# Sliding-window attention and a gated feed-forward on one core: output transposes from the DMA to TensorE, stores to ScalarE's queue

## The chip, the core and the metric

The kernel runs on one core of a Trainium2 chip. The core has five engines, each with its own instruction stream: TensorE (PE, with its weight loads as PEld), VectorE (DVE), ScalarE (ACT), GpSimd (POOL) and SyncE (SP), which here only issues DMAs. The five run side by side and wait for each other by semaphores; an engine takes its own instructions in the order in which they stand. The metric is the device time of one execution in microseconds, as the median of several runs. Before the change it is 388.84 us (three runs: 385.98, 388.84, 389.90).

## What is computed

Eight batches, eight heads, 576 tokens, head size 64. Attention looks back over a window of 128 tokens with a linear bias per head; the result, 4608 tokens of width 512, goes through a gated feed-forward (512 to 2048 to 512). The reference, cut:

```python
scores = scale * np.matmul(q, k.transpose(0, 1, 3, 2))
rel = pos[:, None] - pos[None, :]
bias = slopes[:, None, None] * (-np.abs(rel))[None, :, :]
mask = (rel >= 0) & (rel < 128)
scores = np.where(mask, scores + bias[None], -1e9)
attn = np.exp(scores - scores.max(-1, keepdims=True))
attn = attn / (attn.sum(-1, keepdims=True) + 1e-09)
x = np.matmul(attn, v).transpose(0, 2, 1, 3).reshape(B * S, H * D)
h = x @ w_in
g = h * (1.0 / (1.0 + np.exp(-beta * h)))
return g @ w_out
```

## The kernel before

**Attention.** Each batch has five blocks of tokens (four of 128 rows, one of 64). `load_qk` and `load_v` issue the loads of a block on SP's queue (L92) and have POOL cast them to bf16, into `bst` (L116) or into the value buffer `vs` (L121). `T(b, sb)` transposes a block of q and k into `qkT`: for batches 0 and 1 (`NPE = 2`) by PE with a copy by DVE, for the others by two DMA transposes on SP's queue (L217). `SC(b, m, p)` makes the scores of half a batch (m) for two heads (p) on PE (L257), with ACT's exps (L270) and DVE's mask (L274). `PV(b, qb, g)` multiplies by the values on PE (L296, L300) and normalises on DVE into `xn` (L305, L306). `X(b, qb)` brings a block of outputs, transposed, into the ring `XT`: for batches 0 and 1 by PE and a copy (L323, L328), for the others by a DMA transpose on SP's queue (L319). PSUM tiles `pv`, `xt` and `tps` share two buffers; the scores `sps` have one.

**Feed-forward.** Tokens go in nine groups of 512. `HS(g, j)` is a block of four matmuls over `XT` (L340), then ACT's tanh (L345) and DVE's product (L346) into `gT`; `OS(g, i, n)` is a block of four matmuls over `gT` (L356). Each group has 16 of either. The fourth `OS` of an output tile is followed by ACT's scaling into `osb` (L362) and by the store on SP's queue (L364): 36 stores in all. `hps` has two PSUM buffers, `osb` three in SBUF.

**The order.** PE's order is written by hand: the steps of attention (the list `att`, from batch 1 on) are spread between the blocks of the groups, so that what group g+1 needs stands ahead of it (`need`); in each group the last three to five blocks, and in groups 0 and 1 also the first `lead` blocks, have none. The other engines and the queues are ordered by a scheduler when the program is built. A DMA counts its end on one of eight counters, taken in turn, and so waits for the end of the DMA that stands eight places before it in the whole program.

Of the kernel before, what the change touches and what calls it, by code (L numbers as in the profile page):

```python
# [13 lines left out]
P = 128  # L14
# [3 lines left out]
def kernel(  # L18
# [10 lines left out]
    nc = tc.nc  # L29
    B, H, S, D = q.shape  # L30
# [21 lines left out]
    REF = 64.0  # L52
    NEG = -1e12
    NPE = 2

    const = ctx.enter_context(tc.tile_pool(name="const", bufs=1))
    diff = const.tile([P, P], F32, name="diff")
# [13 lines left out]
    XT = const.tile([P, NDM, XTR], BF16, name="XT")  # L71
# [48 lines left out]
    def load_v(b, sb):  # L120
        return nc.gpsimd.tensor_copy(  # L121
            out=VS[b % 2][0 : ROWS[sb], sb, :, 0:D], in_=load_rows(v, b, sb)
        )
# [88 lines left out]
    def T(b, sb):  # L212
        rows = ROWS[sb]
        src = staged.pop((b, sb))
        if b >= NPE:
            for i in range(2):
                nc.sync.dma_start_transpose(  # L217
                    out=QK[b % 2][:, i, :, P * sb : P * sb + rows],
                    in_=src[0:rows, i].rearrange("r h d -> r (h d)"),
                )  # L220
            return
        tps = psum_t.tile([P, 2, NP, P], BF16, name="tps", tag="t")
        for i in range(2):
            for p in range(NP):
                nc.tensor.transpose(
                    out=tps[:, i, p, :],
                    in_=src[:, i, 2 * p : 2 * p + 2, :].rearrange("r h d -> r (h d)"),
                    identity=ident[:],
                )
        nc.vector.tensor_copy(  # L230
            out=QK[b % 2][:, :, :, P * sb : P * sb + rows], in_=tps[:, :, :, 0:rows]
        )
# [78 lines left out]
    def X(b, qb):  # L311
        nq = ROWS[qb]
        xnv = xns.pop((b, qb))[:].rearrange("p h d -> p (h d)")
        tok0 = (b * S + P * qb) % XTR
        n1 = min(nq, XTR - tok0)
        parts = [(tok0, 0, n1)] + ([(0, n1, nq)] if n1 < nq else [])
        if b >= NPE:
            for at, r0, r1 in parts:
                nc.sync.dma_start_transpose(out=XT[:, :, at : at + r1 - r0], in_=xnv[r0:r1, :])  # L319
            return  # L320
        xt = psum_t.tile([P, NDM, P], BF16, name="xt", tag="t")
        for c in range(NDM):
            nc.tensor.transpose(  # L323
                out=xt[:, c, :], in_=xnv[:, c * P : (c + 1) * P], identity=ident[:]
            )
        copy = nc.vector.tensor_copy if b else nc.scalar.copy
        for at, r0, r1 in parts:
            copy(out=XT[:, :, at : at + r1 - r0], in_=xt[:, :, r0:r1])  # L328
# [21 lines left out]
    def OS(g, i, n):  # L350
        gT = gts[g]
        if n == 0:
            opss[g, i] = psum_o.tile([P, DM], F32, name="ops", tag="ops")
        ops_ = opss[g, i]
        for j in range(4 * n, 4 * n + 4):
            nc.tensor.matmul(  # L356
                ops_[:], lhsT=gT[:, j, i * P : i * P + P], rhs=W2[:, j, :],
                start=(j == 0), stop=(j == NFF - 1),
            )
        if n == 3:  # L360
            osb = osb_pool.tile([P, DM], F32, name="osb", tag="osb")
            nc.scalar.mul(osb[:], ops_[:], 0.5)  # L362
            row0 = g * TOKG + i * P
            nc.sync.dma_start(out=out[row0 : row0 + P, :], in_=osb[:])  # L364


    def merged(a, c):
        n, ia, ic, r = max(len(a), len(c)), 0, 0, []
        for s in range(n):
            while ia < len(a) and ia * n <= s * len(a):  # L370
                r.append(a[ia])
                ia += 1
            while ic < len(c) and ic * n <= s * len(c):
                r.append(c[ic])
                ic += 1
        return r

    def pvx(b, qbs):
        r = []
        for qb in qbs:  # L380
            r += [(None, lambda g=g, qb=qb: PV(b, qb, g)) for g in range(2)]
            if qb != qbs[0]:
                r.append(((b, qb - 1), lambda qb=qb: X(b, qb - 1)))
        r.append(((b, qbs[-1]), lambda: X(b, qbs[-1])))
        return r

    def loads(b, m):

        if b + 1 < B:
            for sb in HALF[m]:  # L390
                load_qk(b + 1, sb)
        if m == 0:
            for sb in (2, 3, 4):
                load_v(b, sb)
        elif b + 1 < B:
            for sb in (0, 1):
                load_v(b + 1, sb)

    HALF = ((0, 1, 2), (3, 4))

    def ts(b, m):
        return [(None, lambda sb=sb: T(b, sb)) for sb in HALF[m]]

    def scs(b, m):
        return [(None, lambda p=p: SC(b, m, p)) for p in range(NP)]
# [5 lines left out]
    att, before = one, []  # L411
    for b in range(2, B):
        for m in range(2):
            nb, nm = (b, 1) if m == 0 else (b + 1, 0)
            if nb < B:
                att += ts(nb, nm)
            att.append((None, lambda b=b, m=m: loads(b, m)))
            att += merged(scs(b, m), before)
            before = pvx(b, ((0, 1), (2, 3, 4))[m])
    att += before  # L420
    place = {key: n + 1 for n, (key, _) in enumerate(att) if key}

# [6 lines left out]
    with tc.manual_schedule(engines={mybir.EngineType.PE}):  # L429

        for sb in range(NQB):
            c = load_v(0, sb)
            if sb == 3:
                with tc.issue_after(c.ins):
                    load_w1(0)
                    load_w1(1)
        for sb in range(3):
            c = load_qk(1, sb)
            if sb:
                with tc.issue_after(c.ins):  # L440
                    load_w1(sb + 1)
        for sb in range(2):
            load_v(1, sb)
        for sb in (3, 4):
            load_qk(1, sb)
        for sb in (2, 3, 4):
            c = load_v(1, sb)
            if sb == 3:
                with tc.issue_after(c.ins):
                    for n in range(4):  # L450
                        load_w2(n)
        with tc.tile_pool(name="psum_x", bufs=2, space=bass.MemoryType.PSUM) as psum_x:
            nsc = 0
            values = [(qb, 0) for qb in range(NQB)]
            for p in range(NP + 1):
                if p < NP:
                    T0(p)
                if p == 1:
                    load_beta()
                if p:  # L460
                    for m in range(2):
                        SC(0, m, p - 1, psum_s if nsc % 3 == 2 else psum_x)
                        nsc += 1
                        if p == NP:
                            PV(0, *values.pop(0))
            for qb, g in values:
                PV(0, qb, g)
        psum_h = ctx.enter_context(
            tc.tile_pool(name="psum_h", bufs=2, space=bass.MemoryType.PSUM))
        psum_o = ctx.enter_context(  # L470
            tc.tile_pool(name="psum_o", bufs=2, space=bass.MemoryType.PSUM))
        for qb in range(NQB):
            c = PV(0, qb, 1)
            if qb:
                X(0, qb - 1)
        X(0, NQB - 1)
        with tc.issue_after(c.ins):
            late_consts()
        for sb in HALF[0]:
            load_qk(2, sb)  # L480
        for sb in (0, 1):
            load_v(2, sb)
        done = 0
        for g in range(NTG):
            items = []
            for j in range(NFF):
                items.append(lambda g=g, j=j: HS(g, j))
                if g > 1:
                    items.append(lambda g=g, j=j: OS(g - 1, j // 4, j % 4))
            if g == 1:  # L490
                for sb in HALF[1]:
                    load_qk(2, sb)
                for _, t in ts(2, 0):
                    t()
                items += [lambda j=j: OS(0, j // 4, j % 4) for j in range(NFF)]
            target = need[g + 1] if g + 1 < NTG else len(att)
            lead = (1, 12)[g] if g < 2 else 0
            start, span_ = done, len(items) - lead - (0 if g == 0 else 5)
            for n, it in enumerate(items):
                it()  # L500
                to = start + (target - start) * (n + 1 - lead) // span_
                while done < min(target, to):
                    att[done][1]()
                    done += 1
        for j in range(NFF):
            OS(NTG - 1, j // 4, j % 4)
# [30 lines left out]
```

## Time and profile before

| | |
|---|---|
| median of three runs | 388.84 us |
| the profiled execution | 389.58 us, its span 387.4 us, mean granted clock 0.932 |
| PE busy | 325.7 us (84% of the span), 2161 matmuls recorded |
| ACT busy | 212.0 us (55%) |
| DVE busy | 187.8 us (48%) |
| POOL busy | 84.7 us (22%) |
| moved by DMA | 52.98 MB, 160222 packets, 149424 of them under 512 B |
| SP's and ACT's queues | 120 loads, 60 score transposes, 31 output transposes and 36 stores on SP's; one load on ACT's |

The span goes from the first to the last instruction; the profiled time lies 2.2 us above it. Busy shares are means over a run with different stages, so the lines that matter are those of a stretch. In the profile, "A <- B" after an idle time names what A waited for. SPq is SP's DMA queue; time there is the time that SP takes to issue. Some matmul records are missing (558 and 555 of 576 each).

### The profile page before, as it was taken

How to read it: one execution, taken by the hardware profiler on the slowest of the kernel's cores; microseconds unless marked ns; L12 is line 12 of the kernel's file. 1: busy time of each engine (PE TensorE's matmuls, PEld its weight loads, DVE VectorE, ACT ScalarE, POOL GpSimd, SP SyncE). 2: the span in 40 equal slices, each digit the busy share in tenths (PEclk: the TensorE clock that was granted, in tenths of full speed). 3: DMA queues.
4: the chain of work that ended last, by engine and by line, in shares of the span. 5: the costliest groups of instructions: out<-in, count | busy, mean ns of one | idle time of the engine just before them, and what ended most of it. 6: DMA issues, size and time to landing. Idle time of an engine off the chain costs nothing.

```text
span 387.4 us, 6060 instructions
## 1 busy us (share of the span) xinstructions
PE 325.7 (84%) x2161; PEld 152.4 (39%) x2201; DVE 187.8 (48%) x409; ACT 212.0 (55%) x407; POOL 84.7 (22%) x139
## 2 busy tenths in 40 slices
PE   3978898767640799989969993899999999999996
PEld 1454454323310244434424441344444445444442
DVE  5474577635210356735635672175666745444310
ACT  3645665677220378656736782277778754445421
POOL 7633623205224132304231242230000000000000
PEclk9979999989685699999999998699999999999999
DMA  7999999869869798949997698983212111201012
GB/s 228 221 212 212 169 192 207 113 129 178 153 141 235 155 196 161 195 98 201 199 186 163 112 239 161 154 164 76 54 60 59 49 34 45 71 28 54 29 55 81
DMA packets 160222, 52.98 MB, mean 137 GB/s; under 512 B 149424, under 2 KB 155584, under 8 KB 160192
## 3 DMA queue, kind: packets, MB, share of 16 engines
q1 hardware_dynamic: 155936, 48.39, 63.5%
q0 software_dynamic: 4224, 4.19, 6.7%
q8 instruction: 17, 0.28, 0.4%
q14 instruction: 13, 0.11, 0.1%
q10 hardware_dynamic: 32, 0.01, 0.0%
HBM read 36.71 MB, written 9.44 MB: 119 GB/s over the span
## 4 chain that ended last, share of the span: by engine, by line
PE 59%; DMA 22%; SPq 14%; issue 2%; POOL 2%; ACT 0%; DVE 0%; POOLq 0%; ACTq 0%
PE ops L356 27%; PE hps L340 25%; DMA fst<-in_v_dram 10%; SPq L92 8%; DMA fst<-in_q_dram 6%; SPq L217 5%; DMA XT<-xn 4%; PE sps L257 3%; DMA fst<-in_k_dram 2%; PE pv L300 2%; PE pv L296 1%; POOL vs L121 1%; SPq L102 1%; SPq L364 1%; POOL bst L116 0%
## 5 line engine op out<-in xcount | busy, mean ns | idle before, releaser
L340 PE MATMUL hps<-XT,W 128*128 128x512 bf16 x558 | 149.2, 391 | 33.1 <-DMA XT<-xn 30.7
L345 ACT ACTIVATE sig<-hps,beta_h 128x512 bf16<-128x512 f32 x144 | 99.6, 692 | 112.1 <-PE hps L340 104.8
L346 DVE SCALAR_TENSOR_TENSOR gT<-sig,hps 128x512 bf16<-128x512 bf16 x144 | 98.5, 684 | 110.9 <-ACT sig L345 110.4
L356 PE MATMUL ops<-W,gT 128*128 128x512 bf16 x555 | 145.0, 388 | 1.4 <-issue 0.9
L340 PEld LDWEIGHTS <-W 128*128 128x128 bf16 x576 | 53.1, 100 | 94.5 <-issue 42.9
L270 ACT ACTIVATE pt<-sps,bias 128x256 bf16<-128x256 f32 (+1 forms) x192 | 75.3, 478 | 24.4 <-PE sps L257 24.2
L356 PEld LDWEIGHTS <-gT 128*128 128x128 bf16 x576 | 53.3, 99 | 60.2 <-issue 5.9
L116 POOL CAST bst<-fst 128x512 bf16<-128x512 f32 (+1 forms) x70 | 44.5, 641 | 146.7 <-DMA fst<-in_q_dram 108.8
L274 DVE TENSOR_TENSOR pt<-pt,mask 128x1024 bf16<-128x1024 bf16 x48 | 34.7, 723 | 22.8 <-ACT pt L270 22.4
L257 PE MATMUL sps<-qkT 64*128 64x256 bf16 (+2 forms) x320 | 27.1, 262 | 11.2 <-DMA qkT<-bst 6.1
L306 DVE TENSOR_TENSOR xn<-pv,zs 128x256 bf16<-128x256 f32 (+1 forms) x80 | 33.7, 422 | 2.5
L121 POOL CAST vs<-fst 128x512 bf16<-128x512 f32 (+1 forms) x40 | 26.0, 652 | 28.4 <-DMA fst<-in_v_dram 27.6
L362 ACT ACTIVATE osb<-ops 128x512 f32<-128x512 f32 x36 | 21.7, 602 | 19.1 <-PE ops L356 18.8
L305 DVE RECIPROCAL zs<-pv 128x4 f32<-128x4 f32 (+1 forms) x80 | 14.2, 177 | 34.8 <-PE pv L300 33.7
L300 PE MATMUL pv<-vs,pt 128*128 128x65 bf16 x320 | 29.6, 197 | 0.2 <-DVE xn L306 0.2
L257 PEld LDWEIGHTS <-qkT 64*128 64x128 bf16 x320 | 11.5, 95 | 40.0 <-issue 35.1
L296 PE MATMUL pv<-vs,pt 128*128 128x65 bf16 x256 | 25.0, 198 | 2.2 <-DVE xn L306 1.7
L300 PEld LDWEIGHTS <-pt 128*128 128x128 bf16 x320 | 22.7, 100 | 9.5 <-issue 0.6
L296 PEld LDWEIGHTS <-pt 128*128 128x128 bf16 x256 | 20.5, 101 | 10.3 <-DVE xn L306 3.4
L265 ACT ACTIVATE pt<-sps 128x1024 bf16<-128x1024 f32 x16 | 15.9, 1025 | 10.7 <-PE sps L257 10.4
L243 PE MATMUL sps<-table,sident 128*128 128x512 bf16 x31 | 10.2, 411 | 1.3 <-ACT pt L265 1.1
L206 DVE COPY qkT<-tps 128x512 bf16<-128x512 bf16 x8 | 5.5, 689 | 7.7 <-PE tps L200 7.7
(41 smaller groups left out, 60.1 us busy)
## 6 DMA issues: line engine op xcount, KB each, us to landing
out_dram<-osb SPq DMA_DIRECT2D x36, 256.0 KB, 2.5
fst<-in_q_dram SPq DMA_DIRECT2D x32, 256.0 KB, 4.6
fst<-in_k_dram SPq DMA_DIRECT2D x32, 256.0 KB, 4.8
fst<-in_v_dram SPq DMA_DIRECT2D x32, 256.0 KB, 5.1
W<-in_moe_w_in_dram POOLq DMA_DIRECT2D x4, 512.0 KB, 8.1
W<-in_moe_w_out_dram POOLq DMA_DIRECT2D x4, 512.0 KB, 11.8
fst<-in_q_dram SPq DMA_DIRECT2D x8, 128.0 KB, 4.2
fst<-in_k_dram SPq DMA_DIRECT2D x8, 128.0 KB, 4.3
```

What stands on the lines that cost most here:

```text
L92: nc.sync.dma_start(out=f[0:rows], in_=src[b, :, P * sb : P * sb + rows, :].rearrange("h p d -> p h d"),)
L116: c = nc.gpsimd.tensor_copy(out=t[0 : ROWS[sb], i], in_=load_rows(src, b, sb))
L257: nc.tensor.matmul(o, lhsT=qk[64 * e : 64 * e + 64, 1, p, P * kb : P * kb + P], rhs=qk[64 * e : 64 * e + 64, 0, p, P * kb : P * kb + nq], ...
L270: nc.scalar.activation(out=pt[:, e, cols], in_=sps[:, e, cols], func=ACTF.Exp, scale=qscale, bias=bias[:, half, h : h + 1],)
L274: nc.vector.tensor_tensor(out=pt[:], in0=pt[:], in1=masks[m][:].rearrange("p (o c) -> p o c", o=1).broadcast_to([P, 2, 512]), op=ALU.mult,)
L296: nc.tensor.matmul(pv[:, hl, 0 : D + 1], lhsT=weights(b, qb - 1, h, 1), rhs=vs[:, qb - 1, h, 0 : D + 1], start=True, stop=False,)
L300: nc.tensor.matmul(pv[:, hl, 0 : D + 1], lhsT=weights(b, qb, h, 0), rhs=vs[:, qb, h, 0 : D + 1], start=qb == 0, stop=True,)
L306: return nc.vector.tensor_tensor(out=xn[0:nq, 4 * g : 4 * g + 4, :], in0=pv[0:nq, :, 0:D], in1=zs[0:nq].broadcast_to([nq, 4, D]), op=ALU.mult,
L340: nc.tensor.matmul(hps[:], lhsT=W1[:, c, bass.ts(j, P)], rhs=XT[:, c, c0 : c0 + TOKG], start=(c == 0), stop=(c == NDM - 1),)
L345: nc.scalar.activation(out=sig[:], in_=hps[:], func=ACTF.Tanh, scale=beta_h[:, j : j + 1])
L346: nc.vector.scalar_tensor_tensor(out=gts[g][:, j, :], in0=sig[:], scalar=1.0, in1=hps[:], op0=ALU.add, op1=ALU.mult)
L356: nc.tensor.matmul(ops_[:], lhsT=gT[:, j, i * P : i * P + P], rhs=W2[:, j, :], start=(j == 0), stop=(j == NFF - 1),)
```

## The change

- `X` uses PE's transposes and a DVE copy for every batch. The DMA branch is gone.
- `T` uses PE for batches 0 to 2 (`NTE = 3`). Batch 2's `T` steps move into the list `att`, merged with its scores, and are no longer issued ahead of group 1's blocks.
- The stores are issued by ACT.
- `loads(b, 0)` issues the last three value blocks of batch b ahead of the q and k of batch b+1.
- The steps of batch 2 end before batch 3's scores begin. `lead` of group 1 is 8 for 12, and the tail without attention is 3 blocks for 5.

```diff
+    NTE = 3
...
-        if b >= NPE:
+        if b >= NTE:
             for i in range(2):
                 nc.sync.dma_start_transpose(
...
-        if b >= NPE:
-            for at, r0, r1 in parts:
-                nc.sync.dma_start_transpose(out=XT[:, :, at : at + r1 - r0], in_=xnv[r0:r1, :])
-            return
         xt = psum_t.tile([P, NDM, P], BF16, name="xt", tag="t")
...
-            nc.sync.dma_start(out=out[row0 : row0 + P, :], in_=osb[:])
+            nc.scalar.dma_start(out=out[row0 : row0 + P, :], in_=osb[:])
...
+        if m == 0:
+            for sb in (2, 3, 4):
+                load_v(b, sb)
         if b + 1 < B:
             for sb in HALF[m]:
                 load_qk(b + 1, sb)
-        if m == 0:
-            for sb in (2, 3, 4):
-                load_v(b, sb)
-        elif b + 1 < B:
-            for sb in (0, 1):
-                load_v(b + 1, sb)
+            if m == 1:
+                for sb in (0, 1):
+                    load_v(b + 1, sb)
...
-            if nb < B:
+            if NTE <= nb < B:
                 att += ts(nb, nm)
             att.append((None, lambda b=b, m=m: loads(b, m)))
-            att += merged(scs(b, m), before)
+            att += merged((ts(b, m) if b < NTE else []) + scs(b, m), before)
             before = pvx(b, ((0, 1), (2, 3, 4))[m])
+        if b < NTE:
+            att += before
+            before = []
...
-                for _, t in ts(2, 0):
-                    t()
...
-            lead = (1, 12)[g] if g < 2 else 0
-            start, span_ = done, len(items) - lead - (0 if g == 0 else 5)
+            lead = (1, 8)[g] if g < 2 else 0
+            start, span_ = done, len(items) - lead - (0 if g == 0 else 3)
```

Line numbers of the new kernel differ by one to three: the loads are L93, DMA score transposes L218, PE's X transposes L320, tanh L342, scaling L359, stores L361.

**SP's queue around batch 3's scores.** Before, from the last transposes of batch 3's q and k (`qkT_74`) to the output transpose that group 2 needs first (rows are DMAs in the order of issue; `fst` is the staging of a load):

```order
L217 DMA_TRANSPOSE qkT_74<-bst 128x4x64 x2
L92 DMA fst<-in_q_dram 128x8x64
L364 DMA out_dram<-osb 128x512
L92 DMA fst<-in_k_dram 128x8x64
L92 DMA fst<-in_q_dram 128x8x64
L92 DMA fst<-in_k_dram 128x8x64
L92 DMA fst<-in_q_dram 128x8x64
L92 DMA fst<-in_k_dram 128x8x64
L92 DMA fst<-in_v_dram 128x8x64 x2
L92 DMA fst<-in_v_dram 64x8x64
L319 DMA_TRANSPOSE XT<-xn 128x4x128
```

The same queue now, from the first transpose of batch 3's q and k to the values behind the last:

```order
L218 DMA_TRANSPOSE qkT_74<-bst 128x4x128 x5
L93 DMA fst<-in_q_dram 128x8x64
L218 DMA_TRANSPOSE qkT_74<-bst 128x4x128
L93 DMA fst<-in_k_dram 128x8x64
L93 DMA fst<-in_q_dram 64x8x64
L93 DMA fst<-in_k_dram 64x8x64
L93 DMA fst<-in_v_dram 128x8x64 x2
L218 DMA_TRANSPOSE qkT_74<-bst 128x4x128 x2
L218 DMA_TRANSPOSE qkT_74<-bst 128x4x64 x2
L93 DMA fst<-in_v_dram 128x8x64 x2
L93 DMA fst<-in_v_dram 64x8x64
```

The store and the output transpose no longer stand between the loads; in the whole program SP's DMAs go from 247 to 170: the 120 loads stay, and 50 of the 60 score transposes.

**ACT's order around the second store.** Before (`pt<-sps` are exps of a score tile, `osb<-ops` the scaling; the waits are those on the engines' and DMAs' counters):

```order
L362 ACTIVATE osb<-ops 128x512 [waits PE_49]
L270 ACTIVATE pt<-sps,bias 128x320 [waits PE_49]
L270 ACTIVATE pt<-sps,bias 128x192
L270 ACTIVATE pt<-sps,bias 128x320
L270 ACTIVATE pt<-sps,bias 128x192
```

And now:

```order
L359 ACTIVATE osb<-ops 128x512 [waits PE_49]
L271 ACTIVATE pt<-sps,bias 128x320 [waits PE_49]
L361 DMA out_dram<-osb 128x512 [waits DMAHW2_49,Activation_49]
L271 ACTIVATE pt<-sps,bias 128x192
L271 ACTIVATE pt<-sps,bias 128x320
L271 ACTIVATE pt<-sps,bias 128x192
```

The store stands between the exps of one score tile. It waits for a DMA counter (`DMAHW2`), and with it the exps behind it. The DMA that used this counter last, eight places before, is one of SP's: for the first store a load of batch 3's fifth block, for the second a score transpose of that block, for the fifteenth a load of batch 7, the 13th from the end of SP's 170 DMAs. From the sixteenth on it is a store.

## The prediction

> **What bounds the kernel now.** I began with the page's forty slices, cut the run into three stretches, and then read the waits of TensorE (PE), the timeline around the longest one, and the rows of the queue that PE waits for.
>
> ```profile
> PE   3978898767640799989969993899999999999996
> PEclk9979999989685699999999998699999999999999
> DMA  7999999869869798949997698983212111201012
> ```
>
> ```profile
> 74.50:129.00 54.50, 25.61 (x171) 11.74 (x175) 13.61 (x29) 19.14 (x46) 15.82 (x24) 0.76 0.95 168
> 129.00:262.00 133.00, 118.72 (x785) 53.39 (x799) 70.77 (x144) 81.08 (x169) 34.56 (x53) 0.93 0.89 169
> 262.00:387.40 125.40, 120.83 (x714) 56.23 (x726) 58.25 (x111) 68.84 (x128) 0.61 (x1) 0.99 0.17 52
> ```
>
> Columns of the stretches: span, busy time of PE, weight loads, DVE, ACT and POOL, granted clock, busy share of the DMA engines, GB/s. From 262 us on PE is busy for 120.83 of 125.40 us at clock 0.99: there PE is the bound, and the other engines keep up. Before that it is idle for 28.9 us in the first stretch and 14.3 us in the second, at a lower clock, while the DMA share is about 0.9. So the time to be won lies between 74 and 262 us.
>
> ```profile
> PE hps L340 <- DMA XT<-xn: 30.7, 4, 17.6
> PE sps L257 <- DMA qkT<-bst: 6.1, 3, 2.7
> PE sps L257 <- ACT pt L270: 4.7, 5, 1.7
> ```
>
> ```profile
> 108.86 5.09 SPq L217 DMA_TRANSPOSE qkT<-bst  x4
> 114.01 0.58 SPq L92 DMA_DIRECT2D fst<-in_q_dram  x1
> ...
> 120.50 3.50 SPq L92 DMA_DIRECT2D fst<-in_v_dram  x3
> ...
> 124.09 1.25 SPq L319 DMA_TRANSPOSE XT<-xn  x1
> ...
> 128.20 1.86 PE L340 MATMUL hps<-XT,W 128*128 128x512 bf16 x4 [17.57 <-DMA XT<-xn]
> ```
>
> (Waits: total us, times, longest; timeline: start, us.) Four waits make 30.7 us: the first matmul of a token group waits for a transposed attention output. In the longest, 17.57 us, the transpose was issued on SP's queue at 124.09, behind four score transposes, a store and nine loads, issued one after the other from 108.86 on. The data was there; the queue was not free.
>
> ```profile
> L217 SPq DMA_TRANSPOSE qkT<-bst x60: 1186/1206/2297, 67.7 to 255.0; - x60
> L319 SPq DMA_TRANSPOSE XT<-xn x20: 1214/1253/1652, 106.2 to 260.8; - x20
> L364 SPq DMA_DIRECT2D out_dram<-osb x17: 373/561/1584, 104.5 to 260.1; - x17
> L92 SPq DMA_DIRECT2D fst<-in_v_dram x28: 433/702/2218, 87.8 to 259.4; - x28
> L92 SPq DMA_DIRECT2D fst<-in_k_dram x26: 425/607/1856, 66.8 to 247.7; - x26
> L92 SPq DMA_DIRECT2D fst<-in_q_dram x25: 425/578/1292, 82.1 to 246.4; - x25
> DMA to landing us min/median/max: 3.1/4.3/6.9
> 67.00:262.00 195.00, 0.89 0.91 168
> 67.72 14.37 SPq L217 DMA_TRANSPOSE qkT<-bst  x10
> ```
>
> These are SP's issues between 67 and 262 us (min/median/max ns; the landing row is that of the loads). At their medians they take 60 x 1.206 + 20 x 1.253 + 17 x 0.561 + 28 x 0.702 + 26 x 0.607 + 25 x 0.578 = 157 of 195 us, and with the long ones most of the rest: SP issues nearly without a pause. The last two rows: the DMA engines are busy for 0.91 of that time, and batch 2's ten score transposes alone hold SP for 14.37 us.
>
> **The change part by part.** *Attention outputs off the DMA.* The 30 X steps of batches 2 to 7 no longer use SP, so the four waits go: -30.7. What could be late instead is DVE's copy, but the order places each X some three blocks of PE work ahead of the group that needs it.
>
> *Batch 2's transposes on PE.* SP saves the 14.37 us, so batch 3's transposes start that much earlier, and the waits of scores for qkT go with them: -6.1 (at the least half, if batch 3 is late again: -3). The five ACT waits of the third row above (4.7) stay; four scores now stand between tanh steps of group 1, so ACT gives 0.69 more to each; I take +1.
>
> *The clock.* After a long wait PE runs its first blocks slowly:
>
> ```profile
> 243.84 1.87 PE hps L340 x4
> 245.70 1.71 PE ops L356 x4
> 247.41 1.71 PE hps L340 x4
> 249.12 1.05 PE ops L356 x4
> ...
> 373.69 10.11 PE ops L356 x46
> ```
>
> A block of four matmuls takes 0.86 us when PE runs freely (the last row: (10.11 - 0.38)/45 = 0.216 each). The four blocks after the wait at 243.84 took 6.34, 2.9 too many. Two other waits (128.20 and 200) have the same tail, and the score waits near 98 a shorter one: -8, between -5 and -10.
>
> *The price on PE.* 30 x 4 + 5 x 8 = 160 transposes.
>
> ```profile
> 32.48 1.06 PE L225 MATMUL tps<-ident,bst 128*128 128x128 bf16 x16
> 72.52 0.39 PE L323 MATMUL xt<-ident,xn 128*128 128x128 bf16 x4
> L225 PE MATMUL tps<-ident,bst x40: 219/219/230, 31.2 to 43.4; 128*128 128x128 bf16 x40
> L328 DVE COPY XT<-xt x5: 283/411/424, 51.6 to 73.2; 128x512 bf16<-128x512 bf16 x4, 128x256 bf16<-128x256 bf16 x1
> L230 DVE COPY qkT<-tps x5: 417/690/692, 31.8 to 43.6; 128x1024 bf16<-128x1024 bf16 x4, 128x512 bf16<-128x512 bf16 x1
> ```
>
> One takes 219 ns by itself, but they overlap: sixteen took 1.06 us, so a further one costs (1.06 - 0.22)/15 = 56 ns, and four in 0.39 say the same. 160 x 0.056 = +9.0, all of it on the path, since PE is to be the bound. The Trainium skill speaks against this: its page "TensorE: Matmul & The Clock Gate", section "Part 4: PE-mode transpose", gives about 275 ns for a transpose inside a kernel. By that the term would be 160 x 0.275 = 44 and the sum 35 higher; the sixteen in 1.06 us decide for 56 ns here. DVE gets 30 x 0.41 + 5 x 0.69 = 15.8 us of copies; in the second stretch it was busy for 70.77 of 133, so they fit: 0.
>
> *Stores on ACT.* SP saves 17 x 0.56 = 10 us. ACT pays for 36 issues.
>
> ```profile
> L140 ACTq DMA_DIRECT2D bflat<-in_moe_beta_dram x1: 438/438/438, 0.7 to 0.7; - x1
> L362 ACT ACTIVATE osb<-ops x36: 597/598/624, 88.2 to 383.9; 128x512 f32<-128x512 f32 x36
> 227.66 0.60 ACT L362 ACTIVATE osb<-ops 128x512 f32<-128x512 f32 x1
> ```
>
> ACT's only DMA issue took 0.438, SP's stores 0.56 at the median: about 18 us in all. ACT is busy for 81.08 of 133, so most of it fits into gaps; behind a store stand exps and tanhs for which PE waits. If the first 15 stores, which fall among exps, delay PE in full, that is 15 x 0.56 = 8; if none does, 0. I take +2, since PE has two buffers there.
>
> *A new wait on ACT.* By the order a store also waits for the DMA eight places earlier, which is now on another queue. If SP is behind, ACT stands still, and then PE. The fifteenth store is the last that waits for a load; that load is the 13th from the end of SP's 170 DMAs. Where is PE then? Before, that store's osb began at 227.66; less the three XT waits up to there (22.5), 6.1 and 5 of clock, plus 15 X and 5 T (5.6): about 200. Where is SP? It needs 195 - 14.4 - 25.1 - 9.5 = 146 us for what is left, so the load is issued at about 67 + 0.9 x 146 = 198 and lands at 203. Bounds: without the long issues 50 transposes x 1.206 + 79 loads x 0.63 = 110, so 67 + 99 + 4 = 170, no wait; if the DMA engines are the limit, 0.91 x 195 = 177 us of work, less a tenth for the transposes taken away (about 3.5 MB of 168 x 0.195 = 32.8), gives 160 and 67 + 144 + 4 = 215, 15 late. Lateness doesn't add up over the stores, it is the largest one that PE pays. A small one comes at once: batch 3's loads are near the first store too. +5, between 0 and 15.
>
> *Values ahead of scores.* Three loads of batch 2 go before six of batch 3: the latter start 3 x 0.7 = 2 us later, but SP is 14 us ahead by then: 0.
>
> Sum on the span of 387.4: -30.7 - 6.1 + 1 - 8 + 9.0 + 2 + 5 = 359.6. The profiled run lies 2.2 above its span and 0.7 above the median of the runs, so I predict 361 us.
>
> **The rivals.**
> (1) *All cover holds*: no new wait, ACT's issues free: 361 - 7 - 3 = 351. For it: SP loses a third of its issues. Against it: the DMA share of 0.91.
> (2) *The DMA engines, not SP, set the pace of the loads*: the stores hold ACT for the full 15, and some of the 8 is paid: 361 + 10 + 5 = 376. For it: the same 0.91.
> (3) *Transposes don't overlap.* With matmuls around them, each could cost PE its whole 219 ns: 160 x 0.219 = 35 in place of 9, and if PE must also wait for the 30 copies because two PSUM buffers serve pv, xt and tps, 30 x 0.41 = 12 more: 399, slower. It decides from 27 us above my sum, that is from 56 + 27000/160 = 225 ns for each. Against it: the four in 0.39 stood between other matmuls. The skill's 275 ns (the page above) would do the same alone: 361 + 35 = 396.
> (4) *The gain is given back*: PE reaches the scores of later batches before their transposes are ready, and XT waits become qkT waits. Behind batch 7's first scores the order has some 430 block matmuls and that batch's attention: 430 x 0.216 + 7 = 100 us. For 385 SP's last transposes would have to land at about 280, later than before (255). With SP's end at 67 + 146 = 213, or 67 + 177 = 244 at its old pace, this sets no limit.
>
> **How the numbers follow.** Main case, 355 to 370: 0.60, predicted 361. Rival 1: 0.10; rival 2: 0.20; rival 3: 0.05; rival 4: 0.05. The range 350 to 379 takes in rival 1's 351 and rival 2's 376 and leaves out 3 and 4 and the edges. About 1% is what a measurement of this kernel tells from no change: faster is under 385.0, slower over 392.7. Faster: 0.60 + 0.10 + 0.20 = 0.90; same 0.05 (rival 4); slower 0.05 (rival 3).
>
> **What would show it.** Right: no wait of hps for a DMA; group 2's first matmul near 104 instead of 128.20; SP's last load near 215 instead of 259; clock near 1 from 75 on; transposes 56 ns apart. The new wait shows as idle ACT between an osb and the exp behind its store, ended by a load. I am wrong if PE stays idle for more than 20 us between 75 and 262, if transposes stand over 200 ns apart, or if hps waits for DVE's XT copies.

## The result and the profile after

The changed kernel takes 369.04 us (median) against 389.37: ratio 0.9486, 95% interval 0.9381 to 0.959. The forecast was 361 with a range of 350 to 379. The direction and the range held, and the time lay 8 us above the forecast. The medians count every execution; the ratio leaves out one slow one on either side (372.41 and 392.04 us). The profiled execution took 370.02 us, its span is 368.2.

These lines are from the page of the new kernel: three of the forty-slice lines (9.2 us a slice) and the group of PE's first feed-forward matmuls (busy us, mean ns, idle before them).

```profile
PE   2978597979698399999998999999999999999995
PEclk9999899989899599999999999999999999999999
DMA  7999999997897999999998934000001100011011
...
L337 PE MATMUL hps<-XT,W 128*128 128x512 bf16 x554 | 146.8, 386 | 3.9 <-DVE gT L343 1.7
```

The same group on the page of the kernel before:

```profile
L340 PE MATMUL hps<-XT,W 128*128 128x512 bf16 x558 | 149.2, 391 | 33.1 <-DMA XT<-xn 30.7
```

The idle time before `hps` falls from 33.1 us to 3.9, and a DMA no longer ends it. The holes in PE's line from the 15th slice on are gone. Behind the first batches two deep ones are left, in the 11th and the 14th slice, and there the clock falls too. The list of waits names what is behind them (total us, times, longest):

```profile
PE sps L258 <- ACT pt L271: 14.2, 6, 6.5
ACT pt L271 <- DMA fst<-in_k_dram: 12.4, 3, 5.8
```

The second row is ACT, about to do exps, ended by a load. ACT does not use that load; only the counter of the stores connects the two. Here is ACT's timeline around the first and the fifth store (start and duration in us, in brackets the idle time before):

```profile
88.65 0.60 ACT L359 ACTIVATE osb<-ops 128x512 f32<-128x512 f32 x1 [2.85 <-PE ops L353]
92.73 0.37 ACTq L361 DMA_DIRECT2D out_dram<-osb  x1
93.15 1.57 ACT L271 ACTIVATE pt<-sps,bias 128x320 bf16<-128x320 f32 x4 [3.91 <-DMA fst<-in_k_dram]
...
117.49 0.62 ACT L359 ACTIVATE osb<-ops 128x512 f32<-128x512 f32 x1
123.50 0.34 ACTq L361 DMA_DIRECT2D out_dram<-osb  x1
123.89 1.57 ACT L271 ACTIVATE pt<-sps,bias 128x256 bf16<-128x256 f32 x4 [5.77 <-DMA fst<-in_k_dram]
```

and PE's at the same places:

```profile
90.31 1.04 PE L353 MATMUL ops<-W,gT 128*128 128x512 bf16 x4
...
94.77 0.40 PE L258 MATMUL sps<-qkT 64*128 64x256 bf16 x6 [3.18 <-ACT pt L271]
...
96.24 1.90 PE L353 MATMUL ops<-W,gT 128*128 128x512 bf16 x4
98.07 0.61 PE L258 MATMUL sps<-qkT 64*128 64x256 bf16 x6
98.61 1.51 PE L353 MATMUL ops<-W,gT 128*128 128x512 bf16 x4
...
108.30 1.03 PE L337 MATMUL hps<-XT,W 128*128 128x512 bf16 x4
...
117.67 0.39 PE L258 MATMUL sps<-qkT 64*128 64x256 bf16 x4 [0.94 <-ACT pt L271]
...
125.50 0.61 PE L258 MATMUL sps<-qkT 64*128 64x256 bf16 x4 [6.47 <-ACT pt L271]
126.05 1.89 PE L353 MATMUL ops<-W,gT 128*128 128x512 bf16 x4
127.87 0.61 PE L258 MATMUL sps<-qkT 64*128 64x256 bf16 x4
128.41 1.89 PE L337 MATMUL hps<-XT,W 128*128 128x512 bf16 x4
130.09 1.15 PE L353 MATMUL ops<-W,gT 128*128 128x512 bf16 x4
```

An output tile is scaled, its store then stands still on ACT, the exps behind it stand with it, and PE waits for the exps because the scores have one PSUM buffer. The three gaps are 3.18 + 0.94 + 6.47 = 10.6 us. The slow rows behind them, each against the 1.04 and 0.39 of the same form at full clock, add 0.86 + 0.22 + 0.47 = 1.6 and 0.22 + 0.85 + 0.22 + 0.85 + 0.11 = 2.3. Together that is 14.5 us by this trace alone. The clock shows in three stretches after the second wait (us of PE, PEld, DVE, ACT and POOL with counts, then clock, DMA share, GB/s):

```profile
124.00:128.00 4.00, 2.50 (x10) 0.69 (x11) 1.53 (x3) 3.60 (x9) 1.82 (x3) 0.50 0.89 181
128.00:132.00 4.00, 4.00 (x17) 1.49 (x14) 1.83 (x3) 2.25 (x5) 0.62 (x1) 0.71 0.87 180
132.00:136.00 4.00, 3.95 (x34) 1.82 (x34) 2.26 (x6) 3.35 (x8) 2.48 (x4) 1.00 1.34 208
```

A gap in one trace is not yet a loss: it counts only as far as PE would not have waited there without the stores on ACT. That, and what each other part is worth, the runs have to tell.

### The profile page after: what moved, and what is told of

It reads as the page before. It is cut to its first block, busy times and chain, and to the rows that moved or that the text cites. A ratio compares the mean times of both kernels' runs of the same rounds, so it can differ in the third digit from the quotient of the medians.

```text
span 368.2 us, 6281 instructions
## 1 busy us (share of the span) xinstructions
PE 329.0 (89%) x2318; PEld 159.1 (43%) x2361; DVE 199.9 (54%) x445; ACT 211.6 (57%) x407; POOL 83.8 (23%) x139
## 4 chain that ended last, share of the span: by engine, by line
PE 41%; DMA 31%; SPq 20%; POOL 3%; issue 2%; ACT 0%; DVE 0%; ACTq 0%; POOLq 0%
PE ops L353 20%; PE hps L337 16%; DMA fst<-in_k_dram 15%; SPq L93 13%; DMA fst<-in_v_dram 11%; SPq L218 6%; DMA fst<-in_q_dram 6%; PE sps L258 2%; POOL bst L117 2%; POOL vs L122 1%; SPq L103 1%; PE pv L301 1%; PE xt L320 1%; PE pv L297 1%; POOL W L170 1%
## 5 line engine op out<-in xcount | busy, mean ns | idle before, releaser
L337 PE MATMUL hps<-XT,W 128*128 128x512 bf16 x554 | 146.8, 386 | 3.9 <-DVE gT L343 1.7
L342 ACT ACTIVATE sig<-hps,beta_h 128x512 bf16<-128x512 f32 x144 | 98.9, 691 | 87.9 <-PE hps L337 71.1
L337 PEld LDWEIGHTS <-W 128*128 128x128 bf16 x576 | 51.6, 99 | 59.1 <-issue 9.5
L353 PEld LDWEIGHTS <-gT 128*128 128x128 bf16 x576 | 52.4, 99 | 56.2 <-issue 4.5
L275 DVE TENSOR_TENSOR pt<-pt,mask 128x1024 bf16<-128x1024 bf16 x48 | 33.9, 705 | 24.7 <-ACT pt L271 24.6
L258 PE MATMUL sps<-qkT 64*128 64x256 bf16 (+2 forms) x320 | 26.7, 262 | 14.6 <-ACT pt L271 14.2
L359 ACT ACTIVATE osb<-ops 128x512 f32<-128x512 f32 x36 | 21.7, 603 | 25.1 <-PE ops L353 24.9
L258 PEld LDWEIGHTS <-qkT 64*128 64x128 bf16 x320 | 11.5, 96 | 43.4 <-issue 41.9
L301 PE MATMUL pv<-vs,pt 128*128 128x65 bf16 x320 | 28.4, 194 | 0.2 <-DVE xn L307 0.2
L297 PE MATMUL pv<-vs,pt 128*128 128x65 bf16 x256 | 23.9, 193 | 2.6 <-DVE xn L307 2.2
L301 PEld LDWEIGHTS <-pt 128*128 128x128 bf16 x320 | 21.5, 97 | 9.3 <-DVE xn L307 0.3
L297 PEld LDWEIGHTS <-pt 128*128 128x128 bf16 x256 | 19.6, 98 | 9.9 <-DVE xn L307 3.6
L266 ACT ACTIVATE pt<-sps 128x1024 bf16<-128x1024 f32 x16 | 15.9, 1025 | 11.2 <-PE sps L258 11.1
L325 DVE COPY XT<-xt 128x512 bf16<-128x512 bf16 (+1 forms) x36 | 13.6, 386 | 10.4 <-PE xt L320 10.3
L320 PE MATMUL xt<-ident,xn 128*128 128x128 bf16 x160 | 15.3, 219 | 1.0 <-DVE xn L307 0.7
```

The lines of the kernel that those rows point to most:

```text
L258: nc.tensor.matmul(o, lhsT=qk[64 * e : 64 * e + 64, 1, p, P * kb : P * kb + P], rhs=qk[64 * e : 64 * e + 64, 0, p, P * kb : P * kb + nq], ...
L275: nc.vector.tensor_tensor(out=pt[:], in0=pt[:], in1=masks[m][:].rearrange("p (o c) -> p o c", o=1).broadcast_to([P, 2, 512]), op=ALU.mult,)
L297: nc.tensor.matmul(pv[:, hl, 0 : D + 1], lhsT=weights(b, qb - 1, h, 1), rhs=vs[:, qb - 1, h, 0 : D + 1], start=True, stop=False,)
L301: nc.tensor.matmul(pv[:, hl, 0 : D + 1], lhsT=weights(b, qb, h, 0), rhs=vs[:, qb, h, 0 : D + 1], start=qb == 0, stop=True,)
L337: nc.tensor.matmul(hps[:], lhsT=W1[:, c, bass.ts(j, P)], rhs=XT[:, c, c0 : c0 + TOKG], start=(c == 0), stop=(c == NDM - 1),)
L342: nc.scalar.activation(out=sig[:], in_=hps[:], func=ACTF.Tanh, scale=beta_h[:, j : j + 1])
```

## The experiments

Theory A: the transposes took SP's queue off PE's path as forecast, and the new wait of the stores on ACT gave some 14 us back. Rivals: the issues on ACT cost by themselves (B), or the loads are limited by the DMA engines and would hold up something else anyway. Each run states its median and its ratio to the kernel before, which took 389.1 to 389.4 us beside them.

**Stores back on SP, or on POOL.**

```diff
-            nc.scalar.dma_start(out=out[row0 : row0 + P, :], in_=osb[:])
+            nc.sync.dma_start(out=out[row0 : row0 + P, :], in_=osb[:])
```

> The changed kernel with the stores back on SP, all else kept. Theory A (the missing 8 us went into two waits of ACT: a store on ACT holds the exps behind it until a load of SP's queue has landed, 3.18 and 6.47 us of PE): the two waits are gone, SP gets some 15 stores between loads (0.56 each) but PE's data were far ahead, so 355 to 365 us, and no exp waits for a load. Rival B (the loads come too late whoever issues the stores): PE waits as long at other places, 367 to 373. Rival C (the stores' move was a real part of the gain): SP is late again, 372 to 382.

The second kernel has `nc.gpsimd` in the same place; by the order of the program its stores count on other counters than the loads.

> Stores issued by POOL, whose DMAs count on other counters than SP's. Theory A: no exp waits for a load; the two gaps of PE go (9.6 us and the slow blocks behind them), 354 to 362 us, if POOL's casts behind a store are not late. Rival B (loads too late anyway): 366 to 373. Rival D: POOL, waiting for osb, holds casts and through them SP's transposes: 370 to 385, and PE waits for qkT or vs.

Measured: 354.44 us (0.9101, 0.9019 to 0.9183) on SP and 354.96 (0.9103, 0.9038 to 0.9168) on POOL. Both are some 14 us faster than the change as made. The stretches of the run with stores on SP:

```profile
74.50:104.00 29.50, 25.11 (x217) 13.43 (x221) 16.06 (x36) 17.06 (x41) 10.71 (x15) 1.00 0.82 162
104.00:129.00 25.00, 22.53 (x159) 10.53 (x161) 15.44 (x32) 19.45 (x44) 8.63 (x14) 1.00 0.96 188
129.00:200.00 71.00, 70.38 (x506) 33.59 (x514) 45.48 (x96) 48.61 (x100) 20.04 (x30) 1.00 0.96 182
```

and the same stretches of the change as made:

```profile
74.50:104.00 29.50, 23.83 (x176) 11.46 (x179) 15.85 (x33) 16.66 (x39) 10.51 (x16) 0.88 0.88 180
104.00:129.00 25.00, 17.49 (x118) 7.87 (x119) 9.00 (x20) 10.09 (x22) 8.87 (x14) 0.82 0.94 186
129.00:200.00 71.00, 68.17 (x483) 32.43 (x490) 41.70 (x88) 46.53 (x97) 21.02 (x34) 0.99 1.11 191
```

With the stores on SP the clock is 1.00 from 74.5 to 200 us, and PE gets 376 matmuls done between 74.5 and 129 us where it got 294. The DMA share is 0.82 to 0.96, against 0.88 to 1.11 in the change; yet from 60 us on no DMA and no issue on SP's queue stands in the chain of work that ended last. So the loads are not what limits this kernel.

PE does the same work in the same order in both traces, so its rows can be set side by side. These are the starts of the same five blocks of scores, in us:

| block of scores | change | stores on SP | lag of the change |
|---|---|---|---|
| before the wait at the first store | 89.98 | 87.00 | 2.98 |
| after it | 100.39 | 93.66 | 6.73 |
| before the wait at the fifth store | 117.67 | 110.94 | 6.73 |
| after it | 132.90 | 118.93 | 13.97 |
| after the fifteenth store | 228.27 | 210.50 | 17.77 |

The first 3 us stand before any store and are not the stores' doing. The wait at the first store then costs 3.7 us, the one at the fifth 7.2, and 3.8 more are lost between 133 and 228 us: 14.8 us in all, where the medians say 14.6. The first two waits thus cost 11.0 us and not the 14.5 of the gaps and slow rows above, because with the stores on SP PE waits for exps too, also at these places: 0.45 and 0.62 us at the first, the same 0.94 ahead of the fifth, and twice 0.69 behind it. Its list of waits and one of these rows:

```profile
PE sps L258 <- ACT pt L271: 6.7, 8, 1.9
...
93.66 0.40 PE L258 MATMUL sps<-qkT 64*128 64x256 bf16 x6 [0.62 <-ACT pt L271]
```

Two different issuing engines give the same time, so what counts is not that SP has the stores, but that ACT has not. The Trainium skill, page "DMA: Bandwidth & Descriptors", section "Issuing engines are not separate DMA queues", says that issuing from several engines saves only the sequencer time of the issue. The runs agree as far as SP and POOL go (354.4 and 355.0); what ACT's stores cost is a wait that this section does not speak of.

**Only some of the stores on ACT.** Two kernels split the 36 stores: the first 16 on SP and 20 on ACT, or the first 8 on ACT and 28 on SP.

```diff
+            (nc.sync if g < 4 else nc.scalar).dma_start(out=out[row0 : row0 + P, :], in_=osb[:])
```

> The first 16 stores (groups 0 to 3) are issued by SP again, the other 20 by ACT. Theory A (the changed kernel loses its 14.6 us because ACT's early stores wait for the counter of one of SP's loads or transposes; issuing by itself costs nothing): the later stores find few of SP's DMAs ahead of them, so 353 to 358 us, and no PE gap above 3 us. Rival B (an issue on ACT costs PE its 0.34 us and the delay of the exps or tanhs behind it): 20 of 36 stores still pay, so 14.6 x 20/36 = 8 us stay: 361 to 364. A store between 200 and 215 us can still meet one of SP's last loads under A: that would show as one gap, at most 5 us.

```diff
+            (nc.scalar if g < 2 else nc.sync).dma_start(out=out[row0 : row0 + P, :], in_=osb[:])
```

> Only the first 8 stores (groups 0 and 1) are issued by ACT, the other 28 by SP; all else as changed. Theory A (the loss of the changed kernel comes from those of its stores that meet a counter of SP's late DMAs; its two long PE gaps, 3.2 us at 92 and 6.5 us at 119, stand behind its first and fifth store, with slow blocks after them): most of the 14.6 us is already lost with these 8, so 364 to 370 us. Rival B (every issue on ACT costs about the same, 14.6/36 = 0.4 us): 354.4 + 8 x 0.4 = 357 to 358.

Measured: 358.66 us (0.9219, 0.9163 to 0.9275) and 368.35 (0.9468, 0.9424 to 0.9512). By the medians the first eight stores alone carry 13.9 of the 14.6 us, with intervals of some 2 and 3 us either way on the two times. Of the twenty late ones, the first costs, and the others don't show: this is ACT's timeline in the kernel with twenty on ACT,

```profile
215.78 0.60 ACT L359 ACTIVATE osb<-ops 128x512 f32<-128x512 f32 x1 [0.42 <-PE ops L353]
220.86 0.38 ACTq L361 DMA_DIRECT2D out_dram<-osb  x1
221.34 0.69 ACT L342 ACTIVATE sig<-hps,beta_h 128x512 bf16<-128x512 f32 x1 [4.97 <-DMA fst<-in_v_dram]
```

and PE behind it:

```profile
223.54 0.39 PE L258 MATMUL sps<-qkT 64*128 64x256 bf16 x4 [3.21 <-ACT pt L271]
223.87 1.59 PE L337 MATMUL hps<-XT,W 128*128 128x512 bf16 x4
...
225.71 1.90 PE L353 MATMUL ops<-W,gT 128*128 128x512 bf16 x4
```

It is the gap that was foreseen under A: one wait for one of SP's last loads, 3.21 us of PE and slow rows behind it. (A had said 358 at most and no gap above 3 us; both were passed by a little.) Against the kernel with all stores on SP this trace falls back by 5 us at this wait and by nothing after it; the medians differ by 4.2. Nothing is left for the other nineteen issues: B falls. In the kernel with eight on ACT the two waits are those of the change again:

```profile
PE sps L258 <- ACT pt L271: 14.2, 6, 6.2
ACT pt L271 <- DMA fst<-in_k_dram: 9.9, 2, 5.5
```

Set beside the kernel with stores on SP, its trace loses 5.0 and 6.1 us at these two waits, 0.4 at the eighth store, and nothing behind the later ones, which SP issues. The change, with ACT issuing these too, loses 3.8 us from the eighth store on. So the first eight stores cost some 11.5 us and the next six the rest; the medians are too coarse to show this split.

**Outputs by DMA again**, once with the stores on ACT as changed, once with the stores on SP:

```diff
+        if b >= NPE:
+            for at, r0, r1 in parts:
+                nc.sync.dma_start_transpose(out=XT[:, :, at : at + r1 - r0], in_=xnv[r0:r1, :])
+            return
```

> Outputs of batches 2 to 7 again by DMA transposes on SP; batch 2's q and k on PE, stores on ACT and the order of the loads as changed. My account of the gain (-30.7 and most of the slow clock for X, +7 for its 120 transposes on PE) gives a loss of some 20 to 25 us against the changed kernel: 385 to 395, with PE waiting for XT again. Rival (the gain came from SP's queue being shorter by stores and ten transposes, so that XT would come in time anyway): 365 to 375.

> Stores on SP, and the attention outputs of batches 2 to 7 by DMA transpose again; batch 2's scores on PE and the order of the loads stay as changed. Theory A (X on PE is what takes away most of the waits, since SP's queue was the limit): SP again carries 30 transposes x 1.25 = 38 us plus 36 stores, and hps waits for XT: 375 to 390 us, 20 to 35 above the 354 of the kernel with stores on SP. Rival C (with batch 2's transposes off SP the queue is already fast enough and XT waits were a matter of batch 2 alone): PE saves its 120 x 0.056 = 7 us and pays some XT waits: 350 to 362.

Measured: 375.93 us (0.9617, 0.953 to 0.9703) and 375.62 (0.967, 0.9608 to 0.9731). The first was a miss: only 7 us above the change, not 16 to 26. The second shows why. With X by DMA it makes no difference where the stores are: PE waits for SP's queue in any case, either at `hps` or behind ACT. With the stores on SP the waits are at `hps`:

```profile
PE hps L341 <- DMA XT<-xn: 24.5, 3, 10.4
```

The outputs on PE are thus worth 7 us while ACT's stores wait (375.9 to 369.0) and 21 us when they don't (375.6 to 354.4).

**Batch 2's scores by DMA again**, with the stores on ACT and on SP:

```diff
-    NTE = 3
+    NTE = 2
...
+                for _, t in ts(2, 0):
+                    t()
```

> Batch 2's q and k again by ten DMA transposes on SP, issued ahead of group 1 as before; outputs on PE and stores on ACT as changed. My account: SP is 14 us later from 67 us on, the stores on ACT meet loads that are later still, so ACT's waits grow: 375 to 385. Rival (batch 2's part is worth only its 6 us of score waits less 2 us of transposes on PE): 370 to 375.

> Stores on SP, batch 2's scores of q and k transposed by DMA again, outputs on PE. Theory A (batch 2's ten DMA transposes put SP 14 us back and PE waits for qkT near 98 us and after): 6 waits of scores minus 40 x 0.056 = 2.2 us on PE and some cold clock: 358 to 364 us. Rival (X on PE gives SP enough room, those transposes are hidden): 352 to 355.

Measured: 373.59 us (0.9586, 0.9501 to 0.9671) and 355.91 (0.9141, 0.9091 to 0.9191). Theory A expected 375 or more of the first and 358 or more of the second. The first came out in its rival's range (370 to 375), the second 0.9 us above its rival's (352 to 355). With outputs on PE and stores on SP the ten DMA transposes of batch 2 are nearly hidden: 1.5 us, which the intervals don't tell from zero. The waits of scores that were 6.1 us before are

```profile
PE sps L258 <- DMA qkT<-bst: 2.4, 2, 1.6
```

**The transposes of the outputs done twice** from batch 3 on, stores on SP. The kernel does these 100 transposes a second time into the same place.

```diff
-        for c in range(NDM):
+        for c in list(range(NDM)) * (2 if b > 2 else 1):
```

> Stores on SP, and the PE transposes of the outputs of batches 3 to 7 are done twice (25 blocks x 4 = 100 further transposes, the same result). By 56 ns for each: 5.6 us more than 354.4, 359 to 361. By the 219 ns that one takes alone: 22 more, 375 to 378. By 275 ns: 27 more, 380 to 383. If there is slack on PE at those places: 354 to 356.

Measured: 358.15 us (0.9221, 0.9163 to 0.928), 3.7 above 354.44, or 37 ns for each; the two intervals, some 3 us each, allow the 5.6 us of 56 ns and not the 22 of 219. The traces are finer: the score block at 110.94 us with stores on SP starts at 111.62 here, and the two spans end at 349.9 and 356.2. The lag grows from 0.7 to 6.3 us over the hundred, which is 56 ns for each. Its timeline shows eight in a row, where the change has four in 0.39:

```profile
264.99 0.61 PE L320 MATMUL xt<-ident,xn 128*128 128x128 bf16 x8
```

```profile
L320 PE MATMUL xt<-ident,xn x160: 216/219/230, 23.3 to 319.9; 128*128 128x128 bf16 x160
271.38 0.39 PE L320 MATMUL xt<-ident,xn 128*128 128x128 bf16 x4
```

That is (0.61 - 0.39)/4 = 55 ns for a further one, in the midst of the feed-forward, though each takes 219 by itself.

**One edit of the kernel before at a time**: the outputs of all batches on PE, or the stores on ACT.

```diff
-        if b >= NPE:
-            for at, r0, r1 in parts:
-                nc.sync.dma_start_transpose(out=XT[:, :, at : at + r1 - r0], in_=xnv[r0:r1, :])
-            return
```

> The kernel before with one edit: the outputs of all batches are transposed on PE. Theory (SP's queue was the limit and the 30 output transposes on it were what PE waited for): the 30.7 us of waits of hps for XT go, 8 of slow clock behind them too, 120 transposes cost 6.7: 389.1 - 30.7 - 8 + 6.7 = 357, so 354 to 362. Rival (the gain is given back: the waits of scores for batch 2's and 3's qkT, 6.1 us before, grow since PE comes earlier while SP still issues all 60 score transposes): 363 to 375.

```diff
-            nc.sync.dma_start(out=out[row0 : row0 + P, :], in_=osb[:])
+            nc.scalar.dma_start(out=out[row0 : row0 + P, :], in_=osb[:])
```

> The kernel before with one edit: the stores are issued by ACT. Theory D (one lateness of SP's queue, paid once: where hps waits for XT anyway, ACT's wait for an SP counter falls into the same time, as with outputs by DMA on either side of the stores, 375.9 and 375.6 us): 383 to 392. Rival E (the wait on ACT adds up to the other): 389.1 + 14.6 = 400 to 406.

Measured: 356.95 us (0.918, 0.9136 to 0.9224) and 387.56 (0.9958, 0.9919 to 0.9997). The first edit alone brings 32.4 us, nearly all that any kernel here won and more than the whole change. Its waits of scores for transposes are down to

```profile
PE sps L257 <- DMA qkT<-bst: 2.0, 1, 2.0
```

without batch 2 having been touched. The second edit costs nothing in the kernel before: there its wait falls into a time in which PE waits anyway. Its waits show that ACT is held there too, and that `hps` waits correspondingly less for XT (30.7 before):

```profile
PE hps L340 <- DMA XT<-xn: 18.8, 3, 9.2
...
PE sps L257 <- ACT pt L270: 16.3, 7, 8.6
```

**The old order of loads**, stores on SP (the last three value blocks go behind the q and k of the next batch again):

```diff
-        if m == 0:
-            for sb in (2, 3, 4):
-                load_v(b, sb)
         if b + 1 < B:
...
+        if m == 0:
+            for sb in (2, 3, 4):
+                load_v(b, sb)
+        elif b + 1 < B:
```

> Stores on SP and the loads in the old order (the last three value blocks behind the q and k of the next batch); all else as changed. Theory (the order of these loads was costed at nothing): 353 to 357 us, the same as the 354.4 with the new order. Rival (values late, so PV waits for vs): 358 to 364.

Measured: 353.74 us (0.9079, 0.903 to 0.9127), the same as 354.44 within the intervals. These two are the best kernels of the study: the change without its stores on ACT, in either order of the loads.

The worth of the two moves off SP's queue, by four kernels with stores on SP:

| | outputs by DMA | outputs on PE |
|---|---|---|
| batch 2's scores by DMA | 389.4 (the kernel before) | 357.0 |
| batch 2's scores on PE | 375.6 | 354.4 |

(The lower row has the new order of loads and the new `lead` and tail as well; with those and batch 2 by DMA, outputs on PE give 355.9. With outputs by DMA no run separates batch 2's move from them.) Either move wins more where it is made first, 13.8 and 32.4 us, than after the other, 2.6 and 21.2: 11.2 us of lateness are taken away by both.

## Why the prediction came near, and what failed

*Attention outputs off the DMA, -30.7.* Right. No wait of `hps` for a DMA is left. The edit alone brought 32.4 us; its own terms, -30.7 - 8 of clock + 120 x 0.056 = 6.7, give -32.0.

*Batch 2's transposes, -6.1 + 1 and 2.2 of PE.* The waits went, but not by this step. They fell to 2.0 us as soon as the outputs left the queue. After that the step was worth 1.5 us in place of some 3 forecast. With the stores on ACT it was worth 4.6. The waits of scores for exps, 4.7 us before and forecast at 1 more, are 6.7 with the stores on SP.

*The clock, -8.* Right where nothing holds PE: 1.00 in the three stretches from 74.5 to 200 us with the stores on SP, above. In the change it is 0.88 and 0.82 up to 129, because the new waits have slow rows behind them, as the old ones had.

*160 transposes at 56 ns, +9.0.* Right: 55 ns from eight in a row, and the hundred doubled ones cost 5.6 us between the traces (3.7 between the medians). Neither 219 ns (22 us) nor the 275 ns that the Trainium skill, page "TensorE: Matmul & The Clock Gate", section "Part 4: PE-mode transpose", gives for one inside a kernel (27.5 us for the hundred) is what a further transpose costs here. DVE's copies cost nothing: with the stores on SP `hps` waits once for one of them, 1.1 us, as it did before.

*Stores on ACT, +2 for the issues, nothing lost on SP.* The issues cost too little to be seen (19 of 20 late stores leave no trace), so this was nearer 0. That SP gains 10 us was worth nothing: with the stores back on SP its last load is issued at 217.0 us in place of 212.8, and the kernel is 14.6 us faster.

*The new wait on ACT, +5, between 0 and 15.* This is the term that was mis-sized: taking the stores off ACT again won 14.6 us. That is the upper end of the range, but not for the reason given, so that the range held is in part luck. I asked how late SP would be at the fifteenth store, had the load land at 203 and the store come at about 200, and wrote that lateness doesn't add up over the stores, so that PE pays the largest one. At the fifteenth store there was no wait at all. Its load was issued at 203.76 us and landed 6.0 us later, but PE was later still: the tile was ready at 215.52 and the store went at 215.55. The loss lay at the first and the fifth store, 3.7 and 7.2 us between the traces, where SP was hardly late; and it did add up, for the stores between the eighth and the fourteenth took 3.8 more. The longest of these is the thirteenth, with its tile ready at 196.16 and its store at 198.62; here are ACT's and PE's rows behind it:

```profile
199.28 1.21 ACT L271 ACTIVATE pt<-sps,bias 128x256 bf16<-128x256 f32 x3 [2.76 <-DMA fst<-in_k_dram]
200.53 0.39 PE L258 MATMUL sps<-qkT 64*128 64x256 bf16 x4 [1.52 <-ACT pt L271]
```

The first store waited for the load issued at 88.57, the fifth for the one issued at 119.16; these are the rows of SP's timeline:

```profile
88.57 0.63 SPq L93 DMA_DIRECT2D fst<-in_k_dram  x1
...
119.16 0.63 SPq L93 DMA_DIRECT2D fst<-in_k_dram  x1
```

and, from the view of that source line, the time from issue to landing of the loads in those two moments, each with the one issued just before it (the two loads themselves took the longest, 4.1 and 4.3):

```profile
DMA to landing us min/median/max: 3.8/4.0/4.1
...
DMA to landing us min/median/max: 4.1/4.2/4.3
```

The first load was issued before the output tile was ready (88.65 + 0.60), the second 1.05 us after it (117.49 + 0.62). Most of the two waits (3.49 us from tile to store at the first, 5.39 at the fifth) is the 4.1 to 4.3 us that a load is under way. A store that comes just when the load eight places ahead has been issued pays this even where SP is on time, and a later one can pay again: it is not one lateness. I had the number for it, a landing of 3.1 to 6.9 us among the rows, and used it only to say when the last load would land. I also left the slow rows out of this term, which the old waits had shown.

Without the two terms for ACT's stores the forecast would have been 361 - 7 = 354, and the kernel with its stores on SP took 354.4.

*Values ahead of scores, 0.* Right: 354.4 and 353.7 with the new and the old order.

*The rivals.* (1) All cover holds, 351: this is close to the kernel with stores on SP, not to the change. (2) The DMA engines set the pace, 376: the time went that way, but not by this mechanism. With the stores on SP the DMA share is up to 0.96, and from 60 us on no load stands in the chain of work that ended last. (3) Transposes don't overlap: excluded by the doubled ones. (4) The gain given back at qkT: no such wait of PE is left in the change.

*The signs.* SP's last load was issued at 212.8 us (215 forecast); group 2's first matmul came at 108.30 (104), late by about what the first store's wait cost. The new wait looks as it was described, idle ACT between an `osb` and the exp behind its store, ended by a load.

## What to carry to other kernels

Where DMAs take turns on a few counters, as here, a DMA that is moved to another engine's queue takes its wait for a counter with it: look up which transfer it waits for and what stands behind it on the new engine, and price that at up to the landing time of the transfer (4 us here) at each place where the two may meet, with the slow rows behind a gap on top. Take off what the bound engine would wait there anyway: the gaps and slow rows of the change's own trace came to 14.5 us at two stores that cost 11.0. If the engine is one that the bound engine waits for, put the issue on one that is not (SP or POOL here, 354 in place of 369 us). Edits that relieve the same queue do not add up: alone the two here brought 32.4 and 13.8 us (the latter with the new order of loads, `lead` and tail), together 35.0.

## What was unexpected of the hardware

An idle PE of 3.18 us was enough for slow rows behind it, up to 1.90 us for 1.04; after one of 6.47 us the granted clock was 0.50 in the 4 us from 124, 0.71 in the next 4, and 1.00 only from 132 on. How short a gap leaves the clock alone is not settled: the kernel with stores on SP in the new order of loads has one of 1.91 us and kept 1.00 in the stretch from 74.5 to 104; the one with the old order has a gap of 1.91 us too and was granted 0.94 there. This is its row of that stretch:

```profile
74.50:104.00 29.50, 26.40 (x218) 13.58 (x222) 15.94 (x37) 16.64 (x39) 9.62 (x14) 0.94 0.87 164
```

By its slow rows the gap of 3.18 us cost 1.6 us on top, and that of 6.47 us 2.3.
